# Key ranges of 64 columns, memory rows loaded once per batch, first loads spread over SyncE, GpSimd and ScalarE, and a newly searched order

## The chip, the cores and the metric

The kernel runs on one core of a Trainium2 chip. The metric is the device time of one execution in microseconds (us). The kernel before was timed three times; one further execution was profiled, and its trace is what the rows below come from.

## The reference

Three stages follow each other, all in float32 (the weights come as float64):

```python
# 1. chunked attention: 4 batches, 8 heads, 768 positions, 64 per head, 8 memory rows
for c in range(nc):                                   # chunks of 32
    k_full = concatenate([mem_k, k[l_start:r_end]])   # 8 memory + 16 left + 32 + 8 right = 64 keys
    a = softmax(scale * q_c @ k_full.T)
    out[c] = a @ v_full
# 2. dense layer, 3072 tokens: 512 -> 2048 -> 512
h = x @ w_in;  g = h * tanh(softplus(h));  x = g @ w_out
# 3. eight experts, each token goes to the one with the highest logit
expert_idx = argmax(xn @ en.T / tau)
out[mask] = gate_w[mask, None] * (relu(x[mask] @ w1[e]) @ w2[e])
```

## The kernel before

**Attention.** It works on 24 pairs of query blocks: pair P has 128 queries (two blocks of 64, four chunks of 32) of all 8 heads. For each pair q, k and v are loaded, q and k are transposed on TensorE (`Tq`; `Tk` 0 and 1 for two key ranges, the tiles `kn` and `kn2`), and copied out of PSUM into `qT` and `kT`, which holds 64 keys for each of the four chunks. Then come the scores (`S`, tile `p_S`), the row maximum (`mx`, VectorE), eight exponentials with their sums (`ex`, ScalarE), the normalisation (`rg`, `rc`, `norm`), the transposition of the probabilities (`PT`, `pT`), the product with v (`V`, tile `p_X`) and the split of the result into two float32r parts (`xh`, `xl`) in `xt`. Three pairs make one block of 384 tokens.

**Weights.** The dense weights come as 32 pieces of 512 KB (`raw`). VectorE turns each from float64 into float32 (`sign`, `bias`, `high`, `low`; `sp` is the result), and `hi` and `lo` split it into two float32r parts (`win_h`, `win_l`, `wout_h`, `wout_l`). Pieces 0 and 1 are the `w_in` part of the first two steps of the dense layer, 2 and 3 their `w_out` part, 4 and 5 the `w_in` part of the next two.

**Dense layer.** One step is 128 columns of the 2048 for a block of 384 tokens: `mm_h` (12 matmuls into `p_h`, a PSUM tile of which there are two), a chain of ScalarE and VectorE operations that ends with `g` (the last reader of `p_h`), `gh`, `gl`, and `mm_y` (9 matmuls). The first `mm_h` needs `xl` of pairs 0 to 2 and `lo` of pieces 0 and 1; `mm_h` of step 2 needs the `p_h` that step 0 has used and `lo` of pieces 4 and 5.

**Order.** Every instruction is put out in one fixed order per engine by a planner (class `Plan`): each operation is a job with a cost per engine, a rank and what it depends on; a table `NUDGE` shifts the ranks. While the first `mm_h` has not been put out, the planner fills waits of TensorE with dummy matmuls (`p_fill`). An engine runs its instructions strictly in that order, also those that issue DMAs; a DMA that SyncE or ScalarE issues waits in that engine's queue until an earlier one has landed, since the two together use eight semaphores in turn (GpSimd has eight others).

**First loads.** For pairs 0 to 2 both SyncE and ScalarE issue the loads of q, k and v. The 8 memory rows are loaded with the keys of every pair (`t[0:NMEM]`). The score masks come in a DMA of their own, put out after `k2` of pair 0.

Of the kernel before, what the change touches and what calls it, by code (L numbers as in the profile page):

```python
# [80 lines left out]
LATENCY, START, SLACK = 2000.0, 1100.0, 34.0  # L81
# [3 lines left out]
def between(a, b):  # L85
# [20 lines left out]
    att50=7.77, att51=6.11, att53=-4.95, att54=0.54, att55=-3.17, att56=-6.73, att57=-4.1, att60=-3.01, att61=-136.05,
    att62=4.65, att63=-14.18, att64=-1.36, att66=-2.99, att67=1.14, att70=-9.47, att71=-16.65, att72=7.47, att73=2.03,
    att74=0.95, att75=2.45, att76=1.73, att77=-11.11, e00=-0.24, e01=-12.86, e10=-1.79, e11=-50.42, e20=0.66, e21=3.17,
    e30=1.63, e31=-5.01, e40=13.9, e41=-4.59, e50=-4.17, e51=-7.35, e60=-6.3, e61=-6.57, e70=8.39, e71=28.01, em=14.53,
    hh0=32.08, hh1=-1.14, hh2=0.82, ld00=27.52, ld01=-2.46, ld10=2.16, ld11=-19.55, load0=-1.3, load10=-5.97,  # L110
# [48 lines left out]
class Plan:  # L159
# [5 lines left out]
    def job(self, key, fn, on, rank, after=(), get=(), use=(), lat=130, tiled=False):  # L165
# [5 lines left out]
        self.jobs[key] = dict(fn=fn, on=on, rank=rank + NUDGE.get(part(key), 0), after=list(after), get=list(get), use=list(use), lat=lat, tiled=tiled,  # L171
                              need=[(tag, sum(t == tag for t, _ in get)) for tag in dict(get)])

    def dma(self, key, fn, on, size, rank, after=(), get=(), use=()):

        uses = list(use) + [h for _, h in get]
        self.job(("issue",) + key, fn, on, rank, after, get, use)
        self.job(key, lambda e: None, dict(Q=size / 350), rank, [("issue",) + key], (), uses, lat=LATENCY)
# [5 lines left out]
    def order(self):  # L184
# [8 lines left out]
        self.log = []  # L193
        ready = {k: START for k, n in todo.items() if n == 0}
        while ready:
            cand = {}
            for k, r in ready.items():
# [4 lines left out]
                if r < np.inf:  # L202
                    begin = lambda e: max(r, free.get(e, 0.0), port if shared(k, e) else 0.0)
                    t, e, d = min((begin(e) + d + (d if shared(k, e) else 0), e, d) for e, d in j["on"].items())
                    t = begin(e)

# [57 lines left out]
def attn_moe_moe_kernel(ctx, tc, q, k, v, mem_k, mem_v, w_in, w_out, emb, tau, w1, w2, cst, out, ydbg=None):  # L264
# [36 lines left out]
    def dma(e, out, src):  # L301
        (nc.scalar if e == A else nc.sync).dma_start(out=out, in_=src)
# [36 lines left out]
    def piece(n):  # L339
# [52 lines left out]
        plan.dma(k("load"), load, dict(SP=470), 2 ** 19, r - 4 if n > 3 else 2 * n - 83, [("issue", "load", n - 1)] if n else [], [(raw_tag(n), raw)])  # L392
# [15 lines left out]
    def pairs(P):  # L408
# [15 lines left out]
        vts = [f"w{12 + P}"] if spare else ["vn", "vn"]  # L424
# [23 lines left out]
        def load_k1(e):  # L448
            if not spare:
                tl["kn", P] = att.tile([K1, H, D], F32, tag="kn", bufs=1, name="kn")  # L450
            t = tl["kn", P]
            dma(e, t[0:NMEM], mem_k[b].rearrange("h p d -> p h d"))
            get_keys(e, t, NMEM, w, w + PREV + QB)

        def load_k2(e):
            t = tl["kn2", P] = own(k2t, [K2, H, D], "kn2", bufs=1)
            get_keys(e, t, 0, w + PREV + QB - 8, w + PREV + 2 * QB)

        def load_v(h):
# [22 lines left out]
        def mem(e):  # L482
            t = tl["vn", P] if spare else vall
# [21 lines left out]
        def kT(m):  # L505
            def f(e):
# [110 lines left out]
        small = 350 / 227  # L617
        rows = lambda n: n * 2e3 * small
        edge = bool(edges)
        iss = lambda n, m: {x: 300 * n + 4.8 * m for x in (["SP", A] if first else ["SP"])}  # L620
        k_ = ("k2", P)
        qs, ks, k2s = ("qn", P), ("kn", P), ("kn2", P)
        plan.dma(("q", P), load_q, iss(1, 128), rows(128), L(0), [("issue", "k2", P - 1)] if P > 2 else [], [(qkt[0], qs)])
        plan.dma(("k1", P), load_k1, iss(3 if i == 0 else 2, K1), rows(K1), L(0.1), [("issue", "q", P)], [] if spare else [("kn", ks)], [qs] if spare else [])
        plan.dma(("k2", P), load_k2, iss(2 if i == NQB - 2 else 1, K2), rows(K2), L(0.2), [("issue", "k1", P)], [(k2t, k2s)])
        kh = qs if spare else ks
        vh = [("vn", P, h) for h in range(2)]
        for h in range(2):
            n = 4 + (2 if h in edges else 0)
            plan.dma(("v", P, h), load_v(h), iss(n, 128), rows(128 * 2), L(6 + 0.1 * h) if first else R(0), [("issue", "v", P, 0)] if h and spare else [("issue", "mem0", 0)] if not P else [] if first else [("issue", "v", P, 0)] if h else [("issue", "v", P - 1, 1)],  # L630
                     [(vts[0], vh[0])] if spare and not h else [] if spare or not P and not h else [("vn", vh[h])], vh[:1] if spare and h or not P and not h else [])
# [5 lines left out]
        if i == 0:  # L637
            plan.dma(("mem0", P), mem0, iss(2, 8), 2 ** 14, L(0.5), [("issue", "v", P, 0)] if P else [], [] if P else [("vn", vh[0])], vh[:1] if P else [])
# [987 lines left out]
```

## Time and profile before

| what | value |
|---|---|
| median of 3 runs | 1047.77 us (1045.24 to 1048.47) |
| the profiled execution, its own time | 1047.28 us |
| span of its trace | 1045.4 us |
| mean granted TensorE clock | 0.983 of full speed |
| TensorE busy | 1008.3 us, 96% of the span |
| VectorE busy | 756.5 us, 72% |
| ScalarE busy | 657.7 us, 63% |
| GpSimd busy | 166.7 us, 16% |

The span is what the trace covers; 1.9 us of the execution lie around it. Busy shares are means over stages with different limits, so the rows below go by stretches of the span. Dummy matmuls count as busy TensorE.

### The profile page before, as it was taken

How to read it: one execution, taken by the hardware profiler on the slowest of the kernel's cores; microseconds unless marked ns; L12 is line 12 of the kernel's file. 1: busy time of each engine (PE TensorE's matmuls, PEld its weight loads, DVE VectorE, ACT ScalarE, POOL GpSimd, SP SyncE). 2: the span in 40 equal slices, each digit the busy share in tenths (PEclk: the TensorE clock that was granted, in tenths of full speed). 3: DMA queues.
4: the chain of work that ended last, by engine and by line, in shares of the span. 5: the costliest groups of instructions: out<-in, count | busy, mean ns of one | idle time of the engine just before them, and what ended most of it. 6: DMA issues, size and time to landing. Idle time of an engine off the chain costs nothing. (4 is left out here: it accounts for less than half of the span.)

```text
span 1045.4 us, 23131 instructions
## 1 busy us (share of the span) xinstructions
PE 1008.3 (96%) x8876; PEld 890.7 (85%) x8876; DVE 756.5 (72%) x1611; ACT 657.7 (63%) x1549; POOL 166.7 (16%) x110
## 2 busy tenths in 40 slices
PE   6888999999999999999999999999999999999996
PEld 5767888988888888888888889888889998988995
DVE  2899999667776667657767766978967667777761
ACT  1578888678887777677677678675634333443441
POOL 0000000000000000000000000010136555656541
PEclk9879999999999999999999999999999999999999
DMA  8767652022423102122212100079079878568200
GB/s 182 210 203 212 173 161 67 1 99 55 120 61 95 27 19 72 42 45 67 47 39 65 27 17 32 1 246 328 22 252 377 294 229 273 168 212 272 82 32 23
DMA packets 166641, 129.31 MB, mean 124 GB/s; under 512 B 108530, under 2 KB 137906, under 8 KB 166268
## 3 DMA queue, kind: packets, MB, share of 16 engines
q1 hardware_dynamic: 153706, 110.70, 35.5%
q0 software_dynamic: 4464, 14.95, 3.9%
q10 hardware_dynamic: 8354, 2.11, 1.1%
q8 instruction: 72, 1.18, 0.5%
q14 instruction: 45, 0.37, 0.1%
HBM read 120.06 MB, written 16.52 MB: 131 GB/s over the span
## 5 line engine op out<-in xcount | busy, mean ns | idle before, releaser
L714 PE MATMUL p_h<-xt,win_h 128*128 128x384 f32 x1024 | 269.9, 345 | 6.7 <-DVE rn L743 6.6
L714 PEld LDWEIGHTS p_h<-xt,win_h 128*128 128x128 f32 x1024 | 182.4, 190 | 15.2 <-ACT win_h L317 5.7
L317 ACT CAST ehi<-eraw 128x1024 fp32r<-128x1024 f32 x89 | 93.5, 1051 | 140.5 <-PE p_y L1462 78.2
L714 PE MATMUL p_h<-xt,win_l 128*128 128x384 f32 x512 | 173.2, 338 | 0.0
L760 PE MATMUL p_y<-wout_h,gh 128*128 128x512 f32 x384 | 159.1, 414 | 0.0
L760 PE MATMUL p_y<-wout_h,gl 128*128 128x512 f32 x384 | 152.8, 398 | 0.2 <-DVE gl L751 0.2
L760 PE MATMUL p_y<-wout_l,gh 128*128 128x512 f32 x384 | 152.8, 398 | 0.0
L1344 DVE TENSOR_TENSOR elo<-eraw,ehi 128x1024 fp32r<-128x1024 f32 x89 | 119.2, 1350 | 41.8 <-ACT ehi L317 41.6
L1462 PE MATMUL p_y<-ehi,hh 128*128 128x512 f32 x432 | 142.8, 400 | 0.0
L1372 PE MATMUL p_h<-xs,ehi 128*128 128x256 f32 x704 | 126.1, 280 | 2.4 <-DVE rn L743 2.1
L737 ACT ACTIVATE m<-m,cf 128x384 f32<-128x384 f32 x128 | 79.0, 617 | 59.2 <-DVE m L733 58.6
L1372 PEld LDWEIGHTS p_h<-xs,ehi 128*128 128x128 f32 x704 | 108.7, 188 | 4.6 <-DVE rn L743 2.5
L733 DVE SCALAR_TENSOR_TENSOR m<-sq,rn 128x384 f32<-128x384 f32 x128 | 71.2, 556 | 56.9 <-ACT rn L307 56.2
L1344 POOL TENSOR_TENSOR elo<-eraw,ehi 128x1024 fp32r<-128x1024 f32 x39 | 93.9, 2407 | 78.7 <-ACT ehi L317 47.0
L1372 PE MATMUL p_h<-xs,elo 128*128 128x256 f32 x352 | 98.3, 279 | 0.0
L1462 PEld LDWEIGHTS p_y<-ehi,hh 128*128 128x128 f32 x432 | 81.5, 189 | 18.6
L714 PEld LDWEIGHTS p_h<-xt,win_l 128*128 128x128 f32 x512 | 97.1, 190 | 0.0
L740 DVE SCALAR_TENSOR_TENSOR rn<-m,rn 128x384 f32<-128x384 f32 x128 | 71.4, 558 | 33.6 <-ACT m L737 32.6
L1266 POOL DMA_INDIRECT vn<-y_d,gi x27 | 29.7, 1102 | 413.2 <-PE p_y L760 339.9
L718 ACT ACTIVATE sq<-p_h 128x384 f32<-128x384 f32 x128 | 62.3, 487 | 43.4 <-PE p_h L714 43.2
L760 PEld LDWEIGHTS p_y<-wout_h,gl 128*128 128x128 f32 x384 | 72.8, 190 | 17.9 <-DVE gl L751 0.6
L1462 PE MATMUL p_y<-elo,hh 128*128 128x512 f32 x216 | 85.5, 396 | 0.0
(272 smaller groups left out, 1800.0 us busy)
## 6 DMA issues: line engine op xcount, KB each, us to landing
eraw<-in_moe_w_dram SPq DMA_DIRECT2D x128, 512.0 KB
vn<-in_v_dram SPq DMA_DIRECT2D x164, 56.0 KB
raw<-in_moe_w_in_dram SPq DMA_DIRECT2D x16, 512.0 KB
raw<-in_moe_w_out_dram SPq DMA_DIRECT2D x16, 512.0 KB
y_d<-ysb SPq DMA_DIRECT2D x24, 256.0 KB
qn<-in_q_dram SPq DMA_DIRECT2D x21, 256.0 KB
kn<-in_k_dram SPq DMA_DIRECT2D x18, 176.0 KB
kn<-in_k_dram SPq DMA_DIRECT2D x21, 144.0 KB
```

What stands on the lines that cost most here:

```text
L317: (nc.scalar.copy if e == A else nc.vector.tensor_copy)(out, src)
L714: nc.tensor.matmul(p, w, xt[j][:, a, kk, :], start=(n == 0), stop=(n == len(ops) - 1))
L718: nc.scalar.activation(t, tl["h", s], AF.Tanh, scale=0.5)
L733: nc.vector.scalar_tensor_tensor(t, tl["sq", s], 4.0, tl["rn", s], ALU.add, ALU.mult)
L737: nc.scalar.activation(t, t, AF.Square, bias=c15)
L740: nc.vector.scalar_tensor_tensor(tl["rn", s], tl["m", s], 0.75, tl["rn", s], ALU.add, ALU.mult)
L760: nc.tensor.matmul(yp[yh][t], x[:, c], w[g][:, o, :], start=(first and n == 0), stop=(final and n == 2))
L1266: nc.gpsimd.indirect_dma_start(out=tl["xg", u, a], out_offset=None, in_=y_d[0:T1 * 128, :] if g == 1 else y_d[:, :], in_offset=bass.Indire ...
L1344: engs[e].tensor_sub(tl["elo", j], raw[b, second, c], tl["ehi", j].bitcast(F32))
L1372: nc.tensor.matmul(p[:, o, :], w[:, kk, s], v[:, kk, :], start=(kk == 0 and m == 0), stop=(kk == KDM - 1 and m == 2))
L1462: nc.tensor.matmul(tl["yy", u][a], v[:, kk, s], w[:, k, :], start=(kk == 0 and m == 0), stop=(kk == KEF - 1 and m == 2))
```

## The change

1. The key ranges are cut otherwise: before, range 0 has 8 memory rows and 88 keys, range 1 has 72 keys, 8 of them a second time. After, range 0 has 8 memory rows and 96 keys, range 1 64 keys (72 for pairs 0 to 2). From pair 3 on both ranges live in one tile, whose first 8 partitions keep the memory rows; these are loaded at the first pair of each batch alone.
2. The first loads: ScalarE issues only the memory rows and range 0 of pairs 0 and 1 (5 DMAs; 23 before). GpSimd issues the v rows of pairs 0 and 1 and their first memory rows (20 DMAs; none before). SyncE issues q, range 1, the weights and the v rows of pair 2. The masks come with the identity in the first DMA.
3. The planner now knows that a DMA waits until the one eight places earlier has landed, and the costs of a DMA issue are written anew.
4. The table `NUDGE` has new numbers throughout, so the order differs on every engine from the start to the end of the program.

The numbers of instructions per form stay the same but for these DMAs, the 96 columns of a `Tk` that become 104, one dummy matmul less (150), and who does an operation that several engines can do.

```diff
-LATENCY, START, SLACK = 2000.0, 1100.0, 34.0
+LATENCY, START, SLACK, RING = 2000.0, 1100.0, 34.0, 8
...
-    acta0=5.36, acta1=-1.04, acta2=-4.66, actb0=4.75, ...
+    acta0=-0.6, acta1=-1.74, acta2=38.91, acta3=-92.06, ...
...
-                    begin = lambda e: max(r, free.get(e, 0.0), port if shared(k, e) else 0.0)
+                    begin = lambda e: max(r, free.get(e, 0.0), port if shared(k, e) else 0.0, landed(e, j["dmas"]) if j["dmas"] else 0.0)
...
-        (nc.scalar if e == A else nc.sync).dma_start(out=out, in_=src)
+        {A: nc.scalar, G: nc.gpsimd}.get(e, nc.sync).dma_start(out=out, in_=src)
...
-        K1, K2 = NMEM + PREV + QB, QB + 8
+        K1, K2, KS = NMEM + LEFT + QB + LEFT, NMEM + QB, LEFT + QB + RIGHT
...
-            dma(e, t[0:NMEM], mem_k[b].rearrange("h p d -> p h d"))
-            get_keys(e, t, NMEM, w, w + PREV + QB)
+            if spare or i == 0:
+                dma(e, t[0:NMEM], mem_k[b].rearrange("h p d -> p h d"))
+            get_keys(e, t, NMEM, w, w + K1 - NMEM)
...
-        iss = lambda n, m: {x: 300 * n + 4.8 * m for x in (["SP", A] if first else ["SP"])}
+        iss = lambda n, e="SP": dict(on={e: 430 * n}, dmas=n)
...
-            plan.dma(("v", P, h), load_v(h), iss(n, 128), ...
+            plan.dma(("v", P, h), load_v(h), on={G: 700 * n} if P < 2 else dict(SP=400 * n), dmas=n, ...
...
-    nc.sync.dma_start(out=ident, in_=cst[:, 0:128])
+    nc.sync.dma_start(out=cf[:, 0:128 + 2 * SEEN], in_=cst[:, 0:128 + 2 * SEEN])
```

ScalarE at the program's start. Before, its 23 DMAs are put out around the copies of `kT`, and the first exponentials (`pr,sm<-p_S,mx`) come behind all of them:

```order
L302 DMA kn_146<-in_k_dram 72x8x64
L302 DMA kn_148<-in_k_dram 72x8x64
L302 DMA vn<-in_v_dram 56x4x64 x8
L317 COPY kT<-p_kT 128x4x3x24
L317 COPY kT<-p_kT 128x4x2x32
L317 COPY kT<-p_kT 128x16x8
L302 DMA vn<-in_v_dram 56x4x64 x4
L302 DMA vn<-vn 8x4x256 x2
L317 COPY kT<-p_k_325 128x4x2x32
L317 COPY kT<-p_k_325 128x4x24
L564 ACTIVATE pr,sm<-p_S,mx 128x64 x8
```

After, ScalarE is done with its DMAs before its first copy:

```order
L313 DMA kn<-in_mem_k_dram 8x8x64
L313 DMA kn<-in_k_dram 16x8x64
L313 DMA kn<-in_k_dram 80x8x64
L313 DMA qkn<-in_mem_k_dram 8x8x64
L313 DMA qkn<-in_k_dram 96x8x64
L318 ACTIVATE qT<-p_qT 128x512
L328 COPY kT<-p_kT 128x4x3x32
L328 COPY kT<-p_kT 128x4x2x24
L328 COPY kT<-p_kT 128x16x8
```

What moved: the 12 loads of v and the 2 copies of memory rows have left ScalarE's queue, and `qT` of pairs 0 and 1 has come to it from VectorE.

VectorE, the place where the first weight piece begins (`sign`, `sp<-raw 128x512`). Before, it stands behind the maxima of pairs 0 to 2 and the whole softmax of pair 0:

```order
L553 TENSOR_REDUCE mx<-p_S 128x2x2 x2
L553 TENSOR_REDUCE pr<-p_S 128x2x2 x2
L568 TENSOR_SCALAR sm<-sm 128x4
L571 RECIPROCAL sm<-sm 128x4
L576 TENSOR_TENSOR pr<-pr,sm 128x256
...
L317 COPY pT<-p_PT 128x512
L568 TENSOR_SCALAR pr<-pr 128x4
L357 TENSOR_SCALAR sp<-raw 128x512
```

After, it stands right behind the maxima of pair 1:

```order
L565 TENSOR_REDUCE mx<-p_S 128x2x2 x2
L328 COPY kT<-p_k_254 128x4x56
L328 COPY kT<-p_k_254 128x4x24
L580 TENSOR_SCALAR sm<-sm 128x4
L583 RECIPROCAL sm<-sm 128x4
L588 TENSOR_TENSOR pr<-pr,sm 128x256
L565 TENSOR_REDUCE pr<-p_S 128x2x2 x2
L368 TENSOR_SCALAR sp<-raw 128x512
```

What moved: one of the two `norm` of pair 0, `qT` of the first pairs and the copy `pT` are no longer ahead of the first weight piece on VectorE.

TensorE, just ahead of the first `mm_h` (`p_h<-xt,win_h`). Before, `V` of pair 2 and `Tq` of pair 3 stand there; the lines left out are `V` of pair 1 and dummy matmuls:

```order
L584 MATMUL p_PT<-cf,pr 128x128 x4
...
L603 MATMUL p_X<-pT,vn 64x32 x32
L494 MATMUL p_qT<-cf,qn 128x128 x4
...
L714 MATMUL p_h<-xt,win_h 128x384 x2
L714 MATMUL p_h<-xt,win_l 128x384
```

After, `Tq` and `Tk` of pair 4 and `PT` of pair 3 stand there, and further up `Tk` and `S` of pair 3 (again dummy matmuls are left out):

```order
L505 MATMUL p_k_617<-cf,kn 128x72 x4
...
L553 MATMUL p_S<-kT,qT 32x64 x32
...
L505 MATMUL p_qT<-cf,qn 128x128 x4
...
L615 MATMUL p_X<-pT,vn 64x32 x32
L505 MATMUL p_kT<-cf,kn 128x104 x4
L596 MATMUL p_PT<-cf,pr 128x128 x4
...
L725 MATMUL p_h<-xt,win_h 128x384 x2
L725 MATMUL p_h<-xt,win_l 128x384
```

What moved: more of pair 3's and pair 4's attention stands ahead of the dense layer. Behind the second `mm_h`, too, `Tk` 1 and `S` of pair 4 now come before the third.

## Rows read from the trace of the kernel before

**Rows 1.** Windows by stage; busy us (x instructions), then PEclk, DMA share, GB/s.

```profile
0.00:17.50 17.50, 11.88 (x81) 8.97 (x82) 5.16 (x14) 1.49 (x2) 0.20 (x4) 0.90 0.89 179
17.50:40.00 22.50, 17.52 (x413) 14.49 (x412) 12.02 (x37) 10.62 (x58) 0.00 (x0) 0.85 0.81 212
100.00:150.00 50.00, 48.21 (x674) 42.17 (x674) 48.79 (x116) 42.96 (x131) 2.35 (x3) 1.00 0.70 201
500.00:600.00 100.00, 100.00 (x990) 88.33 (x989) 70.20 (x161) 71.86 (x189) 0.00 (x0) 1.00 0.18 44
```

**Rows 2.** ScalarE's waits from 0 to 45 us, longest first.

```profile
ACT kT L317 <- DMA vn<-in_v_dram: 16.8, 1, 16.8
...
ACT kT L317 <- DMA vn<-vn: 4.1, 1, 4.1
```

**Rows 3.** Timeline from 0 us, all engines: start, us, engine, line, operation.

```profile
9.31 1.88 DVE L317 COPY kT<-p_kT 128x288 f32<-128x288 f32 x6
...
12.73 6.29 ACTq L302 DMA_DIRECT2D vn<-in_v_dram  x8
...
18.73 0.42 DVE L553 TENSOR_REDUCE mx<-p_S 128x4 f32<-128x256 f32 x1 [3.31 <-PE p_S L541]
...
24.38 0.33 ACT L564 ACTIVATE pr<-p_S,mx 128x64 f32<-128x64 f32 x1
...
27.87 0.35 SPq L302 DMA_DIRECT2D kn<-in_mem_k_dram  x1
...
31.37 0.42 DVE L357 TENSOR_SCALAR sp<-raw 128x512 int32<-128x512 int32 x1
...
36.26 0.24 DVE L568 TENSOR_SCALAR pr<-pr 128x4 f32<-128x4 f32 x2
...
38.67 1.14 PE L603 MATMUL p_X<-pT,vn 64*64 64x32 f32 x64
```

**Rows 4.** Windows of 5 us; the same columns as rows 1.

```profile
40.00:45.00 5.00, 5.00 (x101) 4.43 (x99) 4.88 (x12) 2.09 (x6) 0.00 (x0) 1.00 0.48 166
45.00:50.00 5.00, 4.59 (x29) 4.23 (x27) 4.83 (x10) 3.16 (x9) 0.00 (x0) 1.00 0.61 169
50.00:55.00 5.00, 0.39 (x1) 0.42 (x2) 5.00 (x12) 4.56 (x10) 0.00 (x0) 0.90 0.86 252
55.00:60.00 5.00, 5.00 (x19) 4.91 (x19) 5.00 (x11) 3.31 (x7) 0.00 (x0) 0.50 0.22 84
70.00:75.00 5.00, 3.82 (x72) 3.47 (x73) 5.00 (x10) 3.93 (x10) 1.27 (x1) 0.60 0.77 222
```

**Rows 5.** Timeline from 39 us: the dense layer's first steps.

```profile
40.84 0.42 DVE L357 TENSOR_SCALAR sp<-raw 128x512 int32<-128x512 int32 x1
...
41.18 0.42 DVE L614 TENSOR_TENSOR xt<-p_X,xt 128x256 fp32r<-128x256 f32 x1
...
42.17 0.69 DVE L365 SCALAR_TENSOR_TENSOR sp<-raw,sp 128x512 int32<-128x512 int32 x1
...
42.77 0.69 DVE L387 TENSOR_TENSOR win_l<-sp,win_h 128x512 fp32r<-128x512 f32 x1
...
44.82 0.60 PE L714 MATMUL p_h<-xt,win_h 128*128 128x384 f32 x2
...
46.98 0.50 PE L494 MATMUL p_kT<-cf,kn 96*128 96x96 f32 x4
...
54.61 0.98 PE L714 MATMUL p_h<-xt,win_h 128*128 128x384 f32 x2 [5.02 <-DVE rn L743]
...
62.13 0.86 PE L541 MATMUL p_S<-kT,qT 64*32 64x64 f32 x64
```

**Rows 6.** Groups of GpSimd: busy, mean ns of one.

```profile
L689 POOL DMA_DIRECT2D xt<-x_p x1 | 0.8, 766 | 81.8 <-ACT sq L718 81.8
```

**Rows 7.** GpSimd's timeline in the expert stage: its longest issue.

```profile
737.33 2.01 POOL L1488 DMA_INDIRECT out_dram<-yo,si  x1 [11.05 <-DVE ra L1109]
```

**Rows 8.** Windows of 10 us where routing ends and the experts begin.

```profile
700.00:710.00 10.00, 7.75 (x44) 5.90 (x43) 7.49 (x10) 7.01 (x10) 0.00 (x0) 1.00 1.07 376
```

More of the change, by code (lines that the diff above doesn't have):

```diff
@@ L106 @@
[L106 to L110, printed above, removed]
@@ L163, in __init__, with job @@
         self.bufs, self.jobs, self.users, self.getter = bufs, {}, {}, {}
-    def job(self, key, fn, on, rank, after=(), get=(), use=(), lat=130, tiled=False):
+    def job(self, key, fn, on, rank, after=(), get=(), use=(), lat=130, tiled=False, dmas=0):
         uses = list(use) + [h for _, h in get]
@@ L170, in job, with dma @@
             self.getter[h] = key
-        self.jobs[key] = dict(fn=fn, on=on, rank=rank + NUDGE.get(part(key), 0), after=list(after), get=list(get), use=list(use), lat=lat, tiled=tiled,
+        self.jobs[key] = dict(fn=fn, on=on, rank=rank + NUDGE.get(part(key), 0), after=list(after), get=list(get), use=list(use), lat=lat, tiled=tiled, dmas=dmas,
                               need=[(tag, sum(t == tag for t, _ in get)) for tag in dict(get)])
-    def dma(self, key, fn, on, size, rank, after=(), get=(), use=()):
+    def dma(self, key, fn, on, size, rank, after=(), get=(), use=(), dmas=1):
         uses = list(use) + [h for _, h in get]
-        self.job(("issue",) + key, fn, on, rank, after, get, use)
+        self.job(("issue",) + key, fn, on, rank, after, get, use, dmas=dmas)
         self.job(key, lambda e: None, dict(Q=size / 350), rank, [("issue",) + key], (), uses, lat=LATENCY)
@@ L193, in order, with landed @@
         self.log = []
+        rings = {"Pool": [], "SP": []}
+        rings["Activation"] = rings["SP"]
+        def landed(e, n):
+            ring = rings[e]
+            return max([0.0] + [end.get(ring[x], np.inf) - 400 * i for i in range(n) for x in [len(ring) - RING + i] if 0 <= x < len(ring)])
         ready = {k: START for k, n in todo.items() if n == 0}
@@ L233, in order @@
                 port = t + d
+            if j["dmas"]:
+                rings[e] += [k[1:]] * j["dmas"]
             end[k] = t + d + j["lat"]
@@ L629, in pairs @@
             n = 4 + (2 if h in edges else 0)
-            plan.dma(("v", P, h), load_v(h), iss(n, 128), rows(128 * 2), L(6 + 0.1 * h) if first else R(0), [("issue", "v", P, 0)] if h and spare else [("issue", "mem0", 0)] if not P else [] if first else [("issue", "v", P, 0)] if h else [("issue", "v", P - 1, 1)],
-                     [(vts[0], vh[0])] if spare and not h else [] if spare or not P and not h else [("vn", vh[h])], vh[:1] if spare and h or not P and not h else [])
+            plan.dma(("v", P, h), load_v(h), on={G: 700 * n} if P < 2 else dict(SP=400 * n), dmas=n, size=rows(2 * WIN), rank=L(6 + 0.1 * h) if first else R(0),
+                     after=[("issue", "v", P, 0)] if h else [("issue", "load", 1)] if P == 2 else [("issue", "v", P - 1, 1)] if P else [],
+                     get=[] if first else [("vn", vh[h])], use=vh[:1] if spare else [vh[h]] if first else [])
         t1, t2, t3 = (("a", P, n) for n in range(3))
@@ L1558, in attn_moe_moe_kernel @@
     keys()
-    plan.dma(("masks",), lambda e: nc.sync.dma_start(out=cf[:, 128:128 + 2 * SEEN], in_=cst[:, 128:128 + 2 * SEEN]), dict(SP=470), 2 ** 16, -86, [("issue", "k2", 0)])
     p_fill = ps_h.tile([128, 256], F32, tag="h", name="p_fill")
```

81 lines of the change are left out of this document (43 added, 38 removed).

## Prediction

> **What bounds the kernel now.** I read the windows by stage first. From 100 us on TensorE is busy almost without a break at full clock: 48.21 of 50 us between 100 and 150, all of 100 us between 500 and 600 [rows 1]. The matmuls are the same before and after, so in that part the change can give or lose little. The loss lies at the front. From 0 to 40 us TensorE shows 11.88 and 17.52 us busy, but most of that is dummy matmuls; VectorE works 5.16 of 17.5 and 12.02 of 22.5 us, so it is idle for 22.8 us; the DMA engines are at 0.89 and 0.81 of their time, with 179 and 212 GB/s [rows 1].
>
> Next the waits of ScalarE: of its first 24 us it stood 16.8 us behind loads of v and 4.1 us behind copies of the memory rows that it had to issue itself [rows 2]. The timeline shows what hung on that: the maxima of pair 0 ran at 18.73, after a wait of 3.31 us for the scores; the eight loads of v stood in ScalarE's queue from 12.73 on for 6.29 us; the first exponential came at 24.38, some 5 us after its maxima; and the first weight piece, behind the softmax on VectorE, began at 31.37 [rows 3].
>
> The first `mm_h` starts at 44.82. Step 2 starts at 54.61 after 5.02 us of idle TensorE, released by `g` of step 0 on VectorE [rows 5]. From 40 to 60 VectorE is all but full (4.88, 4.83, 5.00 and 5.00 of each 5 us): there it sets the pace. After the idle stretch the granted clock is 0.50 from 55 to 60, the lower of the two levels, 1.2 GHz, and another dip to 0.60 follows a shorter idle time from 70 to 75 [rows 4].
>
> **The change, part by part.** *ScalarE's queue.* Of 23 issues 5 stay, all ahead of its first copy. The 20.9 us of waiting [rows 2] go; what is late next are data and VectorE.
>
> *Data.* I add up what must have landed before `V` of pair 2 by the order of after: 5 loads of q, 6 weight pieces, the keys and v rows of pairs 0 to 2 with the keys of pair 3, memory rows and constants, 7.57 MB together. Before, 17.5 us at 179 GB/s and 22.5 us at 212 GB/s [rows 1] had moved 7.90 MB by 40 us. At that pace 7.57 MB are there at 38.4. Add `V` (1.1 [rows 3]) and four casts and subtractions at 0.34 us (the spacing of the starts at 40.84 and 41.18 [rows 5]), and the first `mm_h` may start at 40.9.
>
> *VectorE.* The first piece lies behind some 2.7 MB, 15.1 us at 179 GB/s [rows 1]; with its landing I put it at 16 instead of the 31.37 at which it was begun [rows 3]. From there to the last `xl` of pair 2 stand: 15 operations `high`, `low` and `lo` at 0.60 (the starts at 42.17 and 42.77 [rows 5]), 9.0 us; 10 `sign`, `bias` and `hi`, 11 casts and subtractions of x, 4 `mx` and 6 `norm`, 31 at 0.34, 10.5 us; 14 small ones at 0.12 and three copies at 0.31 [rows 3], 2.6 us. That is 22.1 us, so 38.1 if nothing stalls. The data are later; I take 41 for the first `mm_h`, 3.8 us earlier than 44.82.
>
> *Step 2.* It waits for `g` of step 0, which before came 9.7 us after the first `mm_h` began [rows 5]. On VectorE `g` was the 18th row behind the last `xl`; now it is the 16th. Two rows less at 0.60 make 8.5 us, so step 2 starts at 49.5, 5.1 us earlier. By then TensorE has also done attention that before came later: `S` of pairs 3 and 4 (0.86 each), three `Tk`, one `Tq` and one `PT` (0.50 each at the price of a `Tk` [rows 5]), 4.2 us. TensorE's lead is 9.3 us.
>
> *What caps it.* VectorE had worked 22.1 us when the first `mm_h` began (5.16, 12.02 and 4.88 [rows 1, 4]). After, it has done about 3.3 us ahead of the first piece and 22.1 behind it, 25.4 us, at 41. Before, it reached 25.4 us at 48.2. Its lead is 7.2 us, and since it stays nearly full through 150 us (48.79 of 50 [rows 1]), a greater lead of TensorE ends in waits for it. I take 8 us, between 7.2 and 9.3.
>
> *GpSimd's issues.* It issues 2 and 10 DMAs for pair 0, then, after a `norm`, 8 for pair 1. The nearest row is its one plain load, 0.77 us [rows 6]: 9.2 us for pair 0, and 6.2 us more, from about 14.5 on (the `norm` in between follows the exponentials of pair 0), for pair 1, so landed at some 23. `V` of pair 1 is due at about 32: by VectorE's count above, 38.1 less the 6 us of rows between its `xl` and the last one; `V` of pair 0 is due at about 25. Bounds: nothing below, since issue time can only delay; above, its longest issue, 2.01 us [rows 7], by which pair 0 is issued at 24 and pair 1 at 41. I take 0.77, since that row is a plain load and the longest one is indirect.
>
> The Trainium skill speaks against this step: SBUF — State Buffer, in the section "A bandwidth-pool intuition that's wrong (but worth ruling out)", says that a load which GpSimd issues takes about 3.1 us in place of 0.62 while VectorE holds the port they share. By it each of these issues would cost up to 2.5 us more (an estimate from that page). No run so far shows such a load beside VectorE; the plain one here was issued at 0.77 us [rows 6].
>
> *Memory rows once per batch, and the new key ranges.* Some 18 short loads fewer, a `Tk` of 104 columns for one of 96: from pair 3 on SyncE is not waited for by a full TensorE, so I put both at nothing; the cover is the dense layer's matmuls, and without it 18 issues at 0.35 us [rows 3] would be 6 us.
>
> *The order behind the start.* With TensorE full [rows 1], a new order can move little. The one place with a loss is where the experts begin, 2.25 us idle of 10 [rows 8]; it may go or double, so ±2 us, which I set to 0.
>
> **Sum.** The profiled execution took 1047.3 us for a span of 1045.4. Less 8 gives 1039.3; the median of the three runs, 1047.8, stands 0.5 higher, so I say **1039.5 us**.
>
> **The rivals.** *A, the data decide.* The transfers were at 0.89 and 0.81 of the engines [rows 1], and three queues feed the same engines. If the pace falls to 179 GB/s throughout, 7.57 MB need 42.3 us, and the first `mm_h` comes at 44.8 as before. The 4.2 us of attention done ahead stay: 1043.3; if VectorE takes those back too, nothing changes, 1047.5. For it speaks the DMA share; against it, that large weight pieces lie later in the queue and move at 252 GB/s between 50 and 55 [rows 4]. The skill says the same in DMA: Bandwidth & Descriptors, "Issuing engines are not separate DMA queues": issuing from several engines saves only issue time. By that, too, the first `mm_h` would follow the bytes.
>
> *B, slower: GpSimd issues too slowly.* Place: the v rows of pair 1. At 2.01 us an issue [rows 7] they land at 43; `V` of pair 1 and the 6 us of VectorE work between its `xl` and that of pair 2 put the first `mm_h` at 50. That is 5.2 us later than before, paid by the 4.2 us moved: about 1048, no change. At 2.5 us they land at 52, the first `mm_h` comes at 59, and the time is 1047.3 + 14.2 - 4.2 = 1057. It decides from about 2.3 us an issue on. Against it: VectorE has little to do before 16 us, and the row nearest is 0.77. The page named above is what makes it more than idle.
>
> *C, more than the cap.* If VectorE's lead grows because ScalarE and GpSimd take more, the half-clock stretch from 55 to 60 (2.5 us lost at 0.50) and that from 70 to 75 (1.5 us of its 3.82, and 1.2 idle) [rows 4] go as well: 9.3 + 2.5 + 2.7 = 14.5 us, 1033.
>
> *D, the change does not do what it says:* the order is made by costs, and if a wait the planner does not know (a load landing later than it thinks) blocks an engine at the start, the lead is lost there: 1045 to 1051.
>
> **How the numbers follow.** A measurement of this kernel tells about 0.3%, 3.1 us, from no change. Chances: the forecast (1036 to 1042) 0.46; C (below 1036) 0.15; A with the moved work kept (1042 to 1044.6) 0.15; A with nothing left, B at 2 us and D within 3.1 us, 0.13; B beyond its point and D above it, 0.11. Faster is 0.46 + 0.15 + 0.15 = 0.76, the same 0.13, slower 0.11. The range leaves out 0.05 below 1031, and above 1048.5 some 0.13; what the bounds of GpSimd's price and of the data's pace give up to 1048 lies in it.
>
> **What would show it.** Right: ScalarE without a DMA wait after 10 us; the first exponential of pair 0 before 15; the first `sign` at 14 to 18; the first `mm_h` at 39 to 43 with step 2 some 8.5 us behind it; VectorE full from about 16 us on; from 150 us on the same rows as before, 7 to 9 us earlier. Wrong: GpSimd's issues of v at over 2 us each, `V` of pair 1 waiting for `vn`, the first `mm_h` at 45 or later, a longer stretch at 1.2 GHz after it, or more than 2 us lost where the experts begin.

## The result and the profile after

The changed kernel took **1029.3 us** (median of 4 runs, 1028.1 to 1032.6) against 1046.5 us before: ratio 0.984, 95% interval 0.981 to 0.988. It is faster, as forecast, but by 17 us where 8 were forecast, and just below the range. The profiled execution took 1028.1 us for a span of 1026.3, 19.1 us less than before's 1045.4; it was the fastest of the four, so the gap of the two traces is 2 us wider than that of the medians.

Windows of the changed kernel, columns as in [rows 1]:

```profile
0.00:17.50 17.50, 12.84 (x205) 10.03 (x206) 5.07 (x17) 9.06 (x40) 8.48 (x17) 1.00 1.04 194
17.50:40.00 22.50, 20.58 (x455) 17.09 (x455) 19.32 (x54) 14.44 (x57) 5.44 (x9) 1.00 1.01 256
...
45.00:50.00 5.00, 2.51 (x74) 1.80 (x73) 4.98 (x10) 4.82 (x12) 0.00 (x0) 0.95 1.14 256
50.00:55.00 5.00, 5.00 (x22) 4.74 (x22) 5.00 (x14) 4.53 (x21) 1.10 (x2) 0.71 0.78 211
55.00:60.00 5.00, 4.65 (x88) 4.21 (x86) 4.97 (x13) 4.72 (x13) 0.60 (x2) 1.00 0.99 330
70.00:75.00 5.00, 5.00 (x86) 4.54 (x84) 5.00 (x15) 3.74 (x11) 0.61 (x1) 1.00 0.98 231
```

From 17.5 to 40 us VectorE works 19.32 of 22.5 us (12.02 before) and the data flow at 256 GB/s (212 before) [rows 1]. The idle time of TensorE, 4.61 us from 50 to 55 before [rows 4], is now 2.49 us from 45 to 50, and the stretch at a low granted clock behind it (the lower level is 1.2 GHz, 0.50) is shorter: it pulls one window down to 0.71, where before a whole window stood at 0.50. The second such stretch, 0.60 from 70 to 75 [rows 4], is gone.

ScalarE's waits from 0 to 45 us, longest first. What stood at the top of [rows 2], 16.8 and 4.1 us for loads of v and memory rows, is not there:

```profile
ACT qT L318 <- PE p_qT L505: 7.1, 4, 3.9
ACT kT L328 <- PE p_kT L505: 2.3, 3, 1.3
ACT kT L328 <- PE p_k L505: 2.2, 2, 1.6
```

Timeline of the changed kernel (columns as in [rows 3]), the rows that answer to [rows 3, 5]:

```profile
2.75 4.33 POOL L313 DMA_DIRECT2D vn<-in_v_dram  x7
...
10.57 0.76 DVE L565 TENSOR_REDUCE mx<-p_S 128x4 f32<-128x256 f32 x2 [3.08 <-PE p_S L553]
...
11.85 0.34 ACT L576 ACTIVATE pr<-p_S,mx 128x64 f32<-128x64 f32 x1
...
15.72 0.42 DVE L368 TENSOR_SCALAR sp<-raw 128x512 int32<-128x512 int32 x1
...
17.75 5.19 POOL L313 DMA_DIRECT2D vn<-in_v_dram  x8
...
41.40 0.59 PE L725 MATMUL p_h<-xt,win_h 128*128 128x384 f32 x2
...
49.61 1.01 PE L725 MATMUL p_h<-xt,win_h 128*128 128x384 f32 x2 [0.34 <-DVE rn L754]
```

The maxima of pair 0 come at 10.57 (18.73 before), the first exponential at 11.85 (24.38), the first weight piece at 15.72 (31.37), the first `mm_h` at 41.40 (44.82) and step 2 at 49.61 (54.61).

**Where the 19.1 us lie.** What TensorE loses in a stretch can be added up from short windows: idle time, and busy time times what the granted clock lacks to 1. Before, from the first `mm_h` to step 2 (44.82 to 54.61) that is 5.0 us, and from step 2 to 150 us it is 15.2 (7.15 idle, 8.05 by the clock). After, it is 2.5 from 41.40 to 49.61, and 5.2 (3.54 idle, 1.67 by the clock) from there to 150. So step 2 comes 5.0 us earlier; behind it 10.0 us less are lost; and the remaining 4.1 us of the 19.1 fit the attention work done ahead, which the prediction had counted at 4.2: TensorE's attention matmuls ahead of step 2 are busy for 20.1 us, 16.1 before. Behind 150 us nothing was gained: 16.7 us lost, 16.0 before. The 10.0 us are what the prediction did not see.

### The profile page after: what moved, and what is told of

Read it like the earlier page. It is cut to its first block, busy times and chain, and to the rows that moved or that the text cites. A ratio compares the mean times of both kernels' runs of the same rounds, so it can differ in the third digit from the quotient of the medians.

```text
span 1026.3 us, 23076 instructions
## 1 busy us (share of the span) xinstructions
PE 998.7 (97%) x8875; PEld 884.3 (86%) x8875; DVE 750.8 (73%) x1583; ACT 671.5 (65%) x1577; POOL 184.8 (18%) x130
## 3 DMA queue, kind: packets, MB, share of 16 engines
HBM read 119.81 MB, written 16.52 MB: 133 GB/s over the span
## 5 line engine op out<-in xcount | busy, mean ns | idle before, releaser
L771 PE MATMUL p_y<-wout_h,gh 128*128 128x512 f32 x384 | 157.0, 409 | 0.3 <-ACT gh L328 0.3
L1355 DVE TENSOR_TENSOR elo<-eraw,ehi 128x1024 fp32r<-128x1024 f32 x89 | 125.5, 1423 | 42.5 <-ACT ehi L328 41.9
L748 ACT ACTIVATE m<-m,cf 128x384 f32<-128x384 f32 x128 | 78.9, 617 | 51.3 <-DVE m L744 49.5
L751 DVE SCALAR_TENSOR_TENSOR rn<-m,rn 128x384 f32<-128x384 f32 x128 | 71.3, 557 | 37.4 <-ACT m L748 36.7
L762 DVE TENSOR_TENSOR gl<-rn,gh 128x384 fp32r<-128x384 f32 x128 | 71.1, 555 | 23.6 <-ACT gh L328 19.9
```

The source lines that it names most:

```text
L748: nc.scalar.activation(t, t, AF.Square, bias=c15)
L751: nc.vector.scalar_tensor_tensor(tl["rn", s], tl["m", s], 0.75, tl["rn", s], ALU.add, ALU.mult)
L762: engs[e].tensor_sub(t, tl["rn", s], tl["gh", s].bitcast(F32))
L771: nc.tensor.matmul(yp[yh][t], x[:, c], w[g][:, o, :], start=(first and n == 0), stop=(final and n == 2))
L1355: engs[e].tensor_sub(tl["elo", j], raw[b, second, c], tl["ehi", j].bitcast(F32))
```

## The experiments

Theories for the 10 us. **T1**: attention of pairs 3 to 5 now stands ahead of the dense layer, so that TensorE does not wait for it later. **T2**: in the dense stage ScalarE and GpSimd have taken operations from VectorE. **T3**: ScalarE's queue, free of loads, does it all. **T4**: what old engine choices cost comes from the start. **T5**: VectorE sets the pace of the first 16 steps, so time follows its work and its waits; this is the prediction's own cap with other numbers in it.

All times are medians. In the table, T0 is the start of the first `mm_h` in the profiled execution, the loss is TensorE's from T0 to 150 us, worked out as above, and the rest is span less T0 less loss. The profiled execution need not be the median one: those of e1 and e3 were the fastest of theirs (2.9 and 4.0 us under the median), those of e2 and e18 the slowest (2.1 and 4.8 us above it), so there the last four columns do not belong to the time on the left.

| kernel | us | ratio to before | interval | T0 | loss | span | rest |
|---|---|---|---|---|---|---|---|
| before | 1046.5 | | | 44.8 | 20.2 | 1045.4 | 980.4 |
| changed | 1029.3 | 0.984 | 0.981 to 0.988 | 41.4 | 7.7 | 1026.3 | 977.2 |
| e1 changed, old table | 1040.6 | 0.995 | 0.993 to 0.997 | 45.7 | 10.0 | 1035.9 | 980.2 |
| e2 before, new table | 1062.2 | 1.015 | 1.013 to 1.017 | 65.5 | 10.1 | 1062.5 | 986.9 |
| e3 old entries, pairs 3 to 5 | 1056.8 | 1.011 | 1.009 to 1.012 | 44.0 | 27.7 | 1050.9 | 979.2 |
| e4 56 old engines | 1039.0 | 0.993 | 0.992 to 0.995 | 45.4 | 13.8 | 1037.2 | 978.0 |
| e5 38 of them, dense stage | 1039.0 | 0.993 | 0.990 to 0.995 | 42.7 | 16.8 | 1038.2 | 978.7 |
| e6 18 of them, start | 1030.3 | 0.984 | 0.982 to 0.986 | 44.0 | 7.9 | 1029.9 | 978.0 |
| e7 attention later | 1066.0 | 1.018 | 1.016 to 1.021 | 47.1 | 35.5 | 1065.9 | 983.3 |
| e8 before, v on GpSimd | 1047.9 | 1.001 | 1.000 to 1.003 | 44.2 | 18.1 | 1044.7 | 982.4 |
| e9 12.2 us more on VectorE | 1037.8 | 0.991 | 0.989 to 0.993 | 43.8 | 15.9 | 1036.5 | 976.8 |
| e10 9.0 us more on ScalarE | 1031.9 | 0.987 | 0.985 to 0.989 | 41.7 | 12.1 | 1030.0 | 976.2 |
| e11 old key ranges | 1031.0 | 0.985 | 0.984 to 0.987 | 42.4 | 9.9 | 1028.6 | 976.3 |
| e12 v on ScalarE | 1033.0 | 0.987 | 0.985 to 0.989 | 47.8 | 8.4 | 1031.5 | 975.3 |
| e13 first 12 of the 38 | 1032.6 | 0.987 | 0.984 to 0.989 | 44.0 | 9.2 | 1030.8 | 977.6 |
| e14 last 26 of the 38 | 1036.1 | 0.991 | 0.989 to 0.993 | 43.4 | 11.6 | 1032.9 | 977.9 |
| e15 before, new engines | 1054.4 | 1.008 | 1.005 to 1.011 | 47.7 | 23.7 | 1050.9 | 979.5 |
| e16 gl on GpSimd | 1035.1 | 0.989 | 0.987 to 0.992 | 42.9 | 11.5 | 1032.9 | 978.6 |
| e17 before, less low | 1046.0 | 0.999 | 0.998 to 1.001 | 44.6 | 18.7 | 1043.1 | 979.8 |
| e18 changed, less low | 1028.2 | 0.982 | 0.980 to 0.983 | 43.9 | 10.7 | 1030.9 | 976.3 |

The intervals of e6, e10 to e13 and e18 overlap that of the changed kernel, and that of e16 just touches it. But for e2 (which loses 22 us behind 150 us, 6 more than before), e7 and e8, the rest is 975 to 981 us while the span varies by 25: to within 6 us, the time is the start plus what TensorE loses up to 150 us. But for e2, the loss moves far more (7.7 to 35.5) than T0 does (41.4 to 47.8), and a late T0 is not lost time by itself: e12 starts 6.4 us later than the changed kernel and is 3.7 us slower.

**Table and loads.** e1 replaces the whole `NUDGE` of the changed kernel by that of before, e2 does the reverse. e3 takes back only the `att3` entries; they are those of pairs 3 to 5, not of the pairs that its expectation names.

```diff
-    ... att30=-0.41, att31=-70.31, att32=-0.58, att33=-1.39, att35=-0.38, att36=-1.67, att37=-67.52, ...
+    ... att30=10.37, att31=0.34, att32=47.85, att33=-6.87, att35=-74.23, att36=5.68, att37=-1.78, ... att34=1.06, ...
```

> The changed kernel with the rank table of before: the new key ranges, the first loads on three queues and the planner's new costs stay. Theory T1 (the extra 9 us come from the order behind the first mm_h: pairs 3 to 5 of the attention ahead of the dense layer, so TensorE no longer waits for them) and theory T2 (they come from operations that VectorE gave to ScalarE and GpSimd) both live in the order, so both expect most of the extra to go: 1037 to 1042, first mm_h at 40 to 43, losses of TensorE between its first mm_h and 150 us back at 14 to 19 us. Theory T3 (ScalarE's queue, free of loads, gives everything by itself): 1028 to 1033.

> The kernel before with the rank table of the changed one: old loads, old key ranges, old planner costs. T3 (the loads give it): ScalarE's DMA waits of 15 to 21 us are there again, the first exponential comes after 20 us, and the time is 1043 to 1050. T1 or T2 alone, without the loads: 1034 to 1041, with the losses behind the first mm_h down to 6 to 10 us although it starts at 44 or later.

> The changed kernel with the entries of before for pairs 3, 11 and 19 (the third group of each row of pairs) in the rank table alone, so that Tq of pair 4, PT of pair 3 and Tk 0 of pair 4 come behind the first mm_h, V of pair 3 behind the second and S of pair 4 behind the third step. T1: TensorE waits for attention behind 45 us again and the granted clock falls in it: 5 to 9 us slower, 1034 to 1038. T2: under 2 us, 1028 to 1032.

e1 gives 1040.6: the new loads, with the new key ranges and planner costs but the old table, keep a third of the gain, and T3 falls. It is not an earlier start: T0 is 45.7, and the loss behind it has gone from 20.2 to 10.0 already (in its fastest execution). e2 gives 1062.2, slower than before, with T0 at 65.5: with the old loads this new order gains nothing. e3 lost 27, where T1 expected 5 to 9; 14 of its 28 us of loss lie from 100 to 150, far behind the work that was moved, so it says that the entries matter, not that T1's mechanism is right.

**Engines.** e4, e5, e6, e13 and e14 keep the changed kernel's order and give listed operations to the engine that did them before; e15 does the reverse to the kernel before.

```diff
+FORCE = {('bias', 9): "Activation", ('rn', 1): "DVE", ('norm', 4, 0): "DVE", ...
...
         for k, e in self.order():
+            e = FORCE.get(k, e)
             (self.jobs[k]["fn"] if k else self.fill)(e)
```

> The changed kernel in its own order, but 56 operations of the first 24 dense steps and first nine pairs done by the engine that did them before (rn, xh, gh, bias, qT, kT, pT, norm, hi, lo). T2: VectorE is later by the 4 to 6 us that it gave away in the first 150 us and TensorE waits for it: 4 to 7 us slower, 1033 to 1037. T1: under 2 us, 1028 to 1032.

> The changed kernel in its own order, with the engines of before for only those 38 of the 56 operations that lie behind the start (pairs 3 to 8, weight pieces from 8 on, rn, gh and gl of the dense steps). T2 (VectorE relieved in the dense stage): first mm_h at 41.4 as in the changed kernel, then TensorE waits more: 4 to 6 us slower, 1033 to 1036. Theory T4 (all of what the old engines cost comes from the start, where the first mm_h came at 45.4): no loss, 1028 to 1031.

> The changed kernel in its own order, with the engines of before for the 18 of the 56 operations that lie at the start (qT, kT, pT, norm, xh of pairs 0 to 2, bias and hi of pieces 1 to 5). T2: the first mm_h at 45, and no more than these 4 us lost, 1032 to 1035. T4: the late start costs the waits behind it too, 1037 to 1040.

> The changed kernel with the engines of before for the first 12 of the 38 operations of run e5 (bias of pieces 9, 10 and 14, rn of step 1, norm of pair 4, xh of pair 3, hi 8 and 13, lo 9, qT and kT of pair 6, pT of pair 5). If the waits of e5 come from the stretch of 45 to 90 us: 4 to 7 us slower, 1033 to 1036. If they come behind it: under 2 us, 1028 to 1031.

> The changed kernel with the engines of before for the other 26 of the 38 operations of run e5 (bias 15 and 16, norm of pair 6, gh, gl and rn from step 6 on, qT, kT and xh of pairs 6 to 8). The complement of e13: 1033 to 1036 if the waits lie behind 90 us, 1028 to 1031 if they lie ahead of it.

> The kernel before in its own order and with its own loads, but the 56 operations done by the engines that do them in the changed kernel. T5 without regard to waits: VectorE has some 6 us less to do by step 16, so 1040 to 1043. If an engine choice only pays in the order it was made for, waits take it back: 1045 to 1052.

e4 and e5 cost 9.7 us each and e6 next to nothing (1.0 us, within overlapping intervals): it lies in the dense stage, and T4 falls. The two halves of e5 cost 3.3 (e13, within overlapping intervals) and 6.8 us (e14), which add up; neither stretch has it alone. But T2's reason does not cover it either. Windows up to the tanh of step 16 (which comes at 134.3 in the changed kernel), first the changed kernel, then e5:

```profile
0.00:134.30 134.30, 121.71 (x1787) 104.54 (x1788) 117.88 (x287) 107.52 (x342) 20.31 (x32) 0.99 0.89 220
```

```profile
0.00:145.20 145.20, 127.22 (x1790) 108.93 (x1791) 119.81 (x291) 107.64 (x337) 22.59 (x32) 0.95 0.84 206
```

By the same step VectorE (the third engine) has worked 119.81 us in e5 against 117.88: 1.9 us more work, 10.9 us more time. The other 9 us are idle time of VectorE. Its waits in e5 from 45 to 150 us, longest first; in the changed kernel they add up to 0.6:

```profile
DVE mx L569 <- PE p_S L557: 2.8, 2, 2.6
DVE m L748 <- ACT rn L322: 2.5, 2, 1.8
DVE sp L380 <- ACT raw L322: 1.3, 1, 1.3
DVE rn L755 <- ACT m L752: 0.7, 1, 0.7
```

So an engine choice costs through who waits for whom. e15, the new engines in the old order, is 8 us slower than before, more than either of its two expectations: in the old order the choice does not pay.

**Attention later.** e7 shifts, in the finished order, all attention jobs of pairs 3 and on.

```diff
...
+        late = lambda t: 3500 * min(1.0, max(0.0, (130000 - t) / 40000))
+        self.order()
+        log = [(t + (late(t) if att(k) else 0), i, e, k) for i, (t, _, e, k) in enumerate(self.log) if k is None or e != "Q"]
+        for _, _, e, k in sorted(log):
```

> The changed kernel with its own engines; in the planner's finished order all attention work of pairs 3 and on (with its loads) is put 3.5 us of planned time later, from the start to 90 us, fading out by 130 us, so that Tk 0 of pair 4 and PT of pair 3 come behind the first two mm_h, and S of pair 4 behind the fourth in place of the second. T1: TensorE waits for attention or for what queues behind it, 4 to 8 us slower, 1033 to 1037. T2: within 2 us, 1028 to 1032.

It costs 36.7 us, five times what T1 expected. TensorE's longest waits of e7 from 45 to 150 us:

```profile
PE p_h L729 <- DVE rn L758: 18.7, 7, 6.2
PE p_y L775 <- ACT gh L332: 3.5, 2, 2.5
```

They are mostly waits not for attention but for the dense chain: in the same stretch VectorE stands in its queue before attention operations whose input TensorE makes later (4.8 us for `p_k`, 4.3 for `p_S`, 3.2 for `p_qT`), and the chain of the dense step stands behind these. The place of attention in the order matters greatly, as T1 says; that TensorE would wait for attention itself is only a small part of it (its waits for attention tiles come to some 3 us).

**Loads.** e8 and e12 change only who issues loads (`FORCE` as above, on the issues of v and memory rows); e11 puts the key ranges of before back.

> The kernel before in its own order, with the 12 loads of v and 2 copies of memory rows that ScalarE issued given to GpSimd's queue, nothing else changed. The prediction's first step (the 20.9 us of ScalarE's DMA waits hold up the start): the first exponential at 19 to 20 in place of 24.4, first mm_h at 41 to 43, 1041 to 1045. T3 (the queue alone gives what the old rank table kept): 1036 to 1040. If it is the order of VectorE (first weight piece behind the softmax of pair 0) and not ScalarE's queue: first mm_h at 44 to 45, 1045 to 1048.

> The changed kernel in its own order, with the 20 issues of v and memory rows for pairs 0 and 1 that GpSimd has put into ScalarE's queue, nothing else changed. If ScalarE's waits for DMAs hold up the start, as the prediction's first step has it: ScalarE waits 10 to 20 us for DMAs, the first exponential comes at 18 to 25 in place of 11.85, and the time grows by 4 to 10 us, 1033 to 1040. If, as the run with v moved to GpSimd in the kernel before suggests, that queue is not what the start waits for: within 2 us, 1028 to 1032.

> The changed kernel in its own order, with the key ranges of before (96 and 72 columns, 8 keys twice) and the memory rows loaded with every pair. The prediction put this part at nothing: within 1.5 us, 1028 to 1031. If the waits of p_k and p_kT for the rows of kn, 2.5 us in all between 45 and 150 us in the changed kernel, grow with the longer loads: 1031 to 1035.

e8 takes 14 of 23 issues out of ScalarE's queue in the kernel before, and the time does not change: 1.001, interval 1.000 to 1.003. ScalarE's waits in it from 0 to 45 us:

```profile
ACT kT L321 <- PE p_kT L498: 13.7, 1, 13.7
ACT kT L321 <- PE p_k L498: 8.2, 1, 8.2
```

The 20.9 us of [rows 2] have become 21.9 us, put down to TensorE's transposes. But e8 does not free the queue alone. First a transpose (Tk 1) of the kernel before, then e8's timeline:

```profile
12.67 0.44 PE L494 MATMUL p_k<-cf,kn 72*128 72x72 f32 x4 [0.64 <-DMA kn<-in_k_dram]
```

```profile
1.38 6.05 POOL L306 DMA_DIRECT2D vn<-in_v_dram  x9 [0.92 <-POOLq L1608]
...
10.30 5.56 ACTq L306 DMA_DIRECT2D kn<-in_k_dram  x3
...
15.90 0.84 ACT L321 COPY kT<-p_kT 128x288 f32<-128x288 f32 x3 [13.65 <-PE p_kT L498]
...
16.86 0.71 PE L498 MATMUL p_k<-cf,kn 72*128 72x72 f32 x4 [0.98 <-DMA kn<-in_k_dram]
```

GpSimd issues v from 1.38 on, where ScalarE had issued it from 12.73 on [rows 3]; the rows of k come later (the transpose that waits for them starts at 16.86 in place of 12.67); and three issues of k still stand in ScalarE's own queue until 15.86, right ahead of its first copy. The first exponential comes at 25.96 (24.38 before). So e8 shows that moving these issues gains nothing by itself; what the queue cost in the kernel before stays open. In e12 ScalarE waits 10.7 us for a DMA again, the first exponential comes at 19.7, and the time grows by 3.7 us (within overlapping intervals), just short of the 4 to 10 that were expected; of the 17 us, some 4 at most hang on that queue in the changed kernel. e11 is 1.7 us slower, with an interval that overlaps the changed kernel's: near nothing, as predicted.

**More and less work on one engine.**

`xx` is a scratch tile that nothing else uses. Behind `g` of steps 0 to 15, e9 has

```diff
+            for _ in range(3 if 0 <= s < 16 else 0):
+                nc.vector.scalar_tensor_tensor(xx, xx, 1.0, xx, ALU.mult, ALU.mult)
```

and ahead of the exponential of the same steps e10 has

```diff
+            for _ in range(2 if 0 <= s < 16 else 0):
+                nc.scalar.activation(xx, xx, AF.Square)
```

e16 gives `gl` of steps 0 to 15 to GpSimd by the table `FORCE`. e17 (the kernel before) and e18 (the changed one) leave `low` out for 16 pieces:

```diff
-            nc.vector.scalar_tensor_tensor(t, tl["raw", n][0], 29, t, ALU.logical_shift_right, ALU.bitwise_or)
+            if not 4 <= n < 20:
+                nc.vector.scalar_tensor_tensor(t, tl["raw", n][0], 29, t, ALU.logical_shift_right, ALU.bitwise_or)
```

> The changed kernel with three extra VectorE operations on a scratch tile of 128x96 behind g in each of the first 16 dense steps, some 0.4 to 0.6 us a step, 6.4 to 9.6 us in all; nothing waits for their result. Theory T5 (VectorE sets the pace of the first 16 steps, so time follows its work and its waits): the time grows by most of what they take, 5 to 9 us, 1034 to 1039. If chains of waits between the engines set the pace and VectorE is only busy, under 3 us, 1029 to 1032.

> The changed kernel with two extra ScalarE operations on a scratch tile of 128x96 ahead of the exponential of each of the first 16 dense steps, some 0.4 to 0.6 us a step, 6.4 to 9.6 us in all; nothing waits for their result. T5 (VectorE alone sets the pace): ScalarE, busy 121.6 of the first 150 us, has room, under 3 us, 1029 to 1032. If VectorE and ScalarE pass work to and fro so closely that either sets the pace: 5 us or more, 1034 to 1040.

> The changed kernel in its own order, with gl of the first 16 dense steps on GpSimd (14 of them were on VectorE, at about 0.47 us each, 6.6 us). T5: VectorE is relieved by up to 6.6 us and time falls by 2 to 6 us, 1023 to 1027. If GpSimd's slower gl (some 1 to 1.3 us) is waited for by mm_y, or VectorE's own operations grow longer beside it: 1029 to 1034.

> The kernel before, which leaves out the operation low (the last three bits of a weight's float32 mantissa) of weight pieces 4 to 19: 16 VectorE operations at about 0.69 us, 11 us less work on VectorE ahead of dense step 20, and nothing given to another engine. T5: most of it comes back as time, 6 to 10 us faster, 1036 to 1041, with step 16 coming 8 to 11 us earlier. If the old order's waits for attention and the late start set the time: under 3 us, 1043 to 1047.

> The changed kernel, which leaves out the operation low of weight pieces 4 to 19: 11 us less work on VectorE. TensorE loses only 7.7 us between its first mm_h and 150 us there, so T5 gives 3 to 7 us, 1022 to 1026. If VectorE no longer sets the pace in the changed kernel: under 2 us, 1027 to 1030.

The groups of the extra operations, first of e9, then of e10 (busy, mean ns, idle before):

```profile
L758 DVE SCALAR_TENSOR_TENSOR xx<-xx 128x96 f32<-128x96 f32 x48 | 12.2, 255 | 1.1
```

```profile
L737 ACT ACTIVATE xx<-xx 128x96 f32<-128x96 f32 x32 | 9.0, 281 | 0.5
```

12.2 us more on VectorE cost 8.4, and 9.0 more on ScalarE 2.6: so far T5 holds. (In e9 the tanh of step 16, which ends the windows below, comes at 146.7, 12.4 us later than in the changed kernel.) In the other direction T5 fails, in the kernel before. e17 takes 8.7 us of work off VectorE ahead of step 16 in the kernel before, and the time stays (0.999, interval 0.998 to 1.001). Windows up to the tanh of step 16, first of the kernel before, then of e17:

```profile
0.00:153.90 153.90, 131.13 (x1785) 111.48 (x1786) 126.58 (x303) 103.51 (x329) 5.07 (x10) 0.91 0.72 194
```

```profile
0.00:152.50 152.50, 129.22 (x1784) 109.84 (x1785) 117.86 (x287) 103.09 (x329) 5.11 (x10) 0.92 0.72 195
```

VectorE worked 117.86 us up to that step in e17 and 117.88 in the changed kernel: the same amount, and step 16 comes at 152.5 and at 134.3. In the old order the amount of VectorE's work does not set the time; 7 of the 8.7 us turn into idle time. One place shows how. VectorE's timeline of e17 around `g` of step 0, for which step 2 waits:

```profile
52.13 0.55 DVE L741 SCALAR_TENSOR_TENSOR rn<-m,rn 128x384 f32<-128x384 f32 x1
53.41 0.36 DVE L311 TENSOR_SCALAR rn<-rn 128x384 f32<-128x384 f32 x1 [0.73 <-ACT rn L727]
53.68 0.55 DVE L744 SCALAR_TENSOR_TENSOR rn<-rn,p_h 128x384 f32<-128x384 f32 x1
```

Ahead of `g` (53.68; 53.92 in the kernel before) stands `rn` of step 1, which waits for ScalarE's exponential of step 1. The time that was freed on VectorE is spent waiting there, and TensorE's wait for step 2 is still 5.0 us. e18 is 1.1 us faster than the changed kernel in the medians, less than the 3 to 7 of T5, and its interval overlaps; by the ratios to before (0.982 and 0.984) it would be 2.7 us. So it does not decide whether less work pays in the changed kernel.

e16 is 5.8 us slower, a little more than expected. First VectorE's groups of the changed kernel from 45 to 134 us, then those of e16 (same operations, other line numbers), then all of its `gl` on GpSimd:

```profile
L380 DVE SCALAR_TENSOR_TENSOR sp<-raw,sp 128x512 int32<-128x512 int32 x19 | 12.9, 681 | 0.0
...
L368 DVE TENSOR_SCALAR sp<-raw 128x512 int32<-128x512 int32 x17 | 7.1, 416 | 0.0
```

```profile
L384 DVE SCALAR_TENSOR_TENSOR sp<-raw,sp 128x512 int32<-128x512 int32 x18 | 13.8, 766 | 0.0
...
L372 DVE TENSOR_SCALAR sp<-raw 128x512 int32<-128x512 int32 x17 | 8.8, 515 | 0.0
```

```profile
L766 POOL TENSOR_TENSOR gl<-rn,gh 128x384 fp32r<-128x384 f32 x16 | 21.8, 1361 | 80.4 <-ACT gh L332 56.0 <-issue 13.1 <-PE p_S L557 4.5
```

With `gl` on GpSimd most of VectorE's operations take longer (681 to 766 ns and 416 to 515 in these groups; the product with `p_h` takes 542 in both), and by step 16 it has worked 120.2 us, more than the 117.9 with `gl`. Nothing was taken off it.

## Why the prediction was half right

- *ScalarE's queue.* That its DMA waits go, and the dates that follow, came as said: first exponential 11.85 (said: before 15), first `sign` 15.72 (said: 14 to 18). That the waits in the queue were the cause is not shown: e8, with 14 of the 23 issues moved, waits as long, but its rows of k are later too; with 20 issues back the changed kernel loses 3.7 us (e12).
- *Data and VectorE at the start.* First `mm_h` 41.4 for 41. Eight runs that left the start all but alone (e5, e9, e10, e11, e13, e14, e16, e18) had it between 41.7 and 44.0, so 41.4 is at the early end of what the start gives, and that it fits to 0.4 us is partly luck. The two terms behind it also missed in opposite ways: at the measured 194 and 256 GB/s the 7.57 MB would be there at 33.8 (an estimate; 38.4 was said), while VectorE, whose work was sized well (22.3 us for 22.1), was not full from 16 us on but idle for 3.4 of the 25.7 us up to the first `mm_h`.
- *Step 2.* 49.6 for 49.5; 4.1 us of attention ahead for 4.2. TensorE's lead there is 9.1 us for 9.3. It rests on the 41.4, so the same luck is in it.
- *What caps it: the step that failed.* The prediction held that VectorE's lead of 7.2 us caps TensorE's, since VectorE stays nearly full, and took 8. No such cap was there: behind step 2 TensorE's loss fell from 15.2 to 5.2 us. VectorE's lead itself was sized well; what failed is that it took the work behind the first `mm_h` as given. From there to the tanh of step 16, first before, then after:

```profile
44.82:153.90 109.08, 96.91 (x1199) 83.77 (x1197) 104.66 (x243) 89.49 (x266) 4.87 (x6) 0.92 0.68 193
```

```profile
41.40:134.30 92.90, 86.88 (x1118) 76.12 (x1116) 92.09 (x213) 82.99 (x246) 6.38 (x7) 0.98 0.83 215
```

Step 16 comes 19.6 us earlier. 7.3 of them are VectorE's idle time ahead of the first `mm_h` (22.9 us before, 15.6 after; this is the lead of 7.2), 3.6 its idle time behind it (4.4 and 0.8 us), and 8.7 are work that the changed kernel does not have on VectorE ahead of step 16. That this work is gone was needed, with 0.8 us of idle time left behind the first `mm_h`; it was not enough, since e17 leaves out as much in the old order and gains nothing. The half clock was part of it: 8.05 us of TensorE's loss before were the granted clock behind idle stretches, 1.67 after.

- *The order behind the start, put at nothing.* With TensorE taken as full, ±2 us where the experts begin was all that was allowed. The stretch from step 2 to 150 us, where 15.2 us were lost before, was left out of this term, though [rows 4] show it; the 10 us lie there. The old table takes 11.3 us of the 17 back (e1), the old engines of the dense stage alone 9.7 (e5).
- *GpSimd's issues.* 4.33 us for seven, with VectorE idle for all but 0.14 of them, and 5.19 for eight, with VectorE busy for 4.34 of them: 0.62 and 0.65 us each (0.77 was assumed). Rival B did not happen. The Trainium skill's page SBUF — State Buffer, in "A bandwidth-pool intuition that's wrong (but worth ruling out)", has about 3.1 us for a load that GpSimd issues while a VectorE copy holds the port they share; no issue of v here shows that.
- *Data (rival A).* Did not decide: 256 GB/s from 17.5 to 40. *Memory rows and ranges at nothing:* e11, 1.7 us within overlapping intervals. The reason given, that TensorE does not wait for SyncE's loads, is not quite so: from 45 to 150 us it waits 2.5 us for rows of k, 1.3 of them ahead of step 2. *Rival C* (1033, 0.15) had the right place, the half-clock stretches, but as its reason VectorE's relief, which by e17 is not enough.

What is shown: the time is T0 and TensorE's loss up to 150 us; in the old order the loss does not fall with the amount of VectorE's work (e17); it changes with order and engine choice (e1, e3, e5, e7), and in e5 and e7 through waits between queues that run in order. What stays open: which single moves of the new table bring the 10 us. e3 and e7 move other work along with attention, and the loss of e5 is spread over both of its halves. That pairs 3 to 5 ahead of the dense layer are the main part is argued, not shown. The planner's account of outstanding DMAs was not tried by itself.

## What to carry to other kernels

An engine that is busy all the time need not be the bound: before taking its work as a cap, look at what its next link waits for, or leave some of its work out and see whether the time moves. Where three engines pass short operations to and fro in fixed orders, count the bound engine's idle time and its low-clock time place by place; a new order can take back most of it, so such losses are not to be carried over into the forecast unchanged. When loads are moved out of a queue, ask what the next instruction there waits for, and whether the move makes other data late: e8 had its waits back under another name.

## What the runs showed of the hardware

- Idle time of TensorE costs more than itself: before, 12.2 us idle from the first `mm_h` to 150 us came with 8.05 us lost to the lower granted clock behind it; in e7 26.3 us idle came with 9.2. The price is not a fixed share of the idle time: in e16 9.9 us idle came with 1.5.
- With 16 operations of 128x384 on GpSimd in place of VectorE, most of VectorE's own grew longer (by 12 and 24% in the two groups shown), and the 16 took 1.36 us each in place of 0.55 (e16). The Trainium skill has it so, in Perfetto Trace Analysis, "Optimizing Scalar/DVE Operations": moving operations between the two may not help, since they share a port to SBUF. The run agrees, and shows that it can cost 5.8 us; that the port is the reason was not tried.
- GpSimd's issues of plain loads were not lengthened by VectorE's work: 0.62 us each from 2.75 on, beside an idle VectorE (busy 0.14 of 4.33 us), and 0.65 from 17.75 on, beside a busy one (4.34 of 5.19 us).
